# One queue for the early transfers, and new places for the steps that prepare the weights

## The chip, the cores and the metric

The kernel runs on one core of a Trainium2 chip. The metric is the device time of one execution in microseconds (us); lower is better. All inputs lie in the chip's memory (HBM) in the layout that the host has prepared, and the core brings them to its on-chip memory by DMA transfers. A transfer is issued by the queue of an engine; here by SyncE (SP in the rows), which does nothing else, and by ScalarE (ACT), which issues transfers in between its activations, in program order. The other engines are TensorE (PE; PEld are its weight loads), VectorE (DVE) and GpSimd (POOL).

## What is computed

Three stages follow one another, for 4 batches, 8 heads, 768 steps and 48 channels a head:

```python
f = 1.0 / (1.0 + np.exp(-f_logit))                       # stage 1: gated linear attention
for t in range(S):
    state = f[:, :, t, :, None] * state + k_t (x) v_t    # outer product
    y[:, :, t] = q_t @ state
h = xt @ U @ V                                           # stage 2, over time, rank 32; x = y
u = x + h.transpose(0, 2, 1)
x = u + np.maximum(u @ w_ch1, 0.0) @ w_ch2               # 384 -> 1536 -> 384
theta = x @ w_theta                                      # stage 3
y = w_tok_r @ (x * np.cos(theta)) + w_tok_i @ (x * np.sin(theta))
u = x + y
out = u + np.maximum(u @ w_ch, 0.0)
```

The weights come in 64 bits and are turned into 32-bit numbers on the chip; the large products use a high and a low part of each operand, three products instead of one.

## The kernel before

**Attention.** The 768 steps of a batch are cut into 6 chunks of 128 (`c`; over all batches they are numbered `g`, 0 to 23). A chunk has one tile `raw` [128, 3, 4, 128]: the q, k and gate rows of four head pairs, even heads on partitions 0 to 47 and odd heads on 64 to 111. `load_raw(g)` fetches it in two halves of 288 KB, one for each set of partitions; for chunk 0 each half is cut once more so that the gate comes first. Four such tiles are in turn in use by the first batch, so chunk 4 goes into chunk 0's tile and chunk 5 into chunk 1's, once the last reader there is done. `load_v(g)` fetches the chunk's `vt`, three buffers in turn. The memsets ahead of the loads clear partitions 32 to 63 of each `raw` tile on VectorE and GpSimd, and two tiles `first` are filled on VectorE.

For each chunk the steps are: `pre_a` (ScalarE: sigmoid of the gates, L232, and two small copies), `pre_s` (VectorE: the running product of the gates as one scan, L241; GpSimd: q times it, L245), `pre_r` four times (VectorE: reciprocal, L252; GpSimd: k times it, L255), `sc` (TensorE: scores, L266), `mask_` twice (VectorE, L277), `kt` (TensorE: transposes of k, L287; ScalarE copies them), `kv` (TensorE: the chunk's addition to the state; ScalarE copies it, L337; GpSimd adds it up), `xx` (TensorE: the chunk's output, L303 and L309; ScalarE copies it to `xf`, L312, and the state to `wst`, L345), `xt` (TensorE: transposes of `xf`, L354; ScalarE copies them), `au` (TensorE: the product with U, L457). `nxt_load(c)`, right after xx(c), issues load_raw of chunk c + 4 and load_v(c + 3) for the first batch's start. Between the steps of batch 0 stand fillers (`keep_warm`, L450): products whose result nobody uses, in numbers that WARM and KEEP give.

**The order** is written out by hand: the instructions of every engine run in the order in which the steps are called. `attention(0)` gives the list of steps of batch 0 with a weight each; `place` runs through it and puts other steps in at given shares of the sum of weights. Those others are the 15 pieces of weights of stage 2: piece 0 is U, 1 and 2 are the halves of V (96 KB each), 3 to 14 are half matrices of 768 KB, alternately of `w_ch1` and `w_ch2`. A piece has four steps, whose places are the four numbers of its row in WPOS: the load (`w_load`, which calls `w_issue`, L739 on, and `fetch`, L865), the scale (two activations on ScalarE, L869 and L871), the join (two instructions on VectorE, L874 and L877, that make 32 bits of 64) and the store (a copy on ScalarE, L166 for the large pieces and L759 for V, with a subtraction on GpSimd, L163). Places of 1 and more stand in the list after it, `moe1(0)`: stage 2 of batch 0, TensorE products with pieces 3 to 14 as weights (L514, L531, L534), with the attention of batch 1 put in between. APOS gives the places of batch 1's first steps in batch 0's list; LN bounds the lane of `hT` (the product with V, L475) of the second half in moe1(0).

A piece is loaded into a slot: pieces 0 and 8 share slot 0, pieces 1, 2 and 9 slot 1, piece 7 has slot 2; the others are loaded over weight tiles that are filled later.

**Who issues what, before.** In load_raw the first halves go out on SyncE, the second halves of batch 0 on ScalarE, those of later batches on SyncE. `vt` goes out on SyncE. Of the pieces, 0 to 7 go out on ScalarE, 8 to 14 on SyncE. load_raw(0) is called inside the loop of memsets, after the first `raw` tile's; load_raw(1) to load_raw(3) with load_v(0) to load_v(2) after that loop. A step that issues a transfer takes its turn in its engine's order, and waits there for the tile to be free.

Of the kernel before, what the change touches and what calls it, by code (L numbers as in the profile page):

```python
# [15 lines left out]
B, H, S, D = 4, 8, 768, 48  # L16
DM = H * D
DFF = 4 * DM
RANK = 32
CH = 128  # L20
NCH = S // CH
# [4 lines left out]
HT = S // 2  # L26
# [42 lines left out]
W0 = (100, 1200, 800, 600)  # L69

WPOS = (
    (0.1827, 0.1862, 0.3967, 0.3987),
    (0.181, 0.3167, 0.4779, 0.5379),
    (0.1871, 0.3096, 0.78, 0.782),
    (0.1954, 0.3485, 0.781, 0.8798),
    (0.4876, 0.6876, 0.8144, 0.8857),
    (0.3106, 0.4606, 0.8355, 0.9329),
    (0.5676, 0.7591, 0.9091, 0.9916),
    (0.5164, 0.6603, 1.02, 1.059),
    (0.5308, 1.15, 1.155, 1.246),  # L80
    (0.784, 1.028, 1.156, 1.247),
    (1.005, 1.187, 1.206, 1.258),
    (0.9349, 1.215, 1.217, 1.295),
    (1.063, 1.28, 1.413, 1.438),
    (1.248, 1.541, 1.554, 1.584),
    (1.258, 1.625, 1.662, 1.758),
)
LN = (0.01438, 0.1137)
AKNOT = (0.0301, 0.2835, 0.5161, 0.6622, 0.8408)
APOS = (0.8165, 0.9293, 0.9293, 0.9577, 0.9577, 0.999)  # L90
P_MIN = 2.0 ** -60
P_FLOOR = 2.0 ** -80

# [23 lines left out]
def place(main, timed):  # L117

    total = sum(w for w, _ in main)
    todo = sorted(timed, key=lambda x: x[0])  # L120
    i, at = 0, 0.0
    for w, f in main:
        while i < len(todo) and todo[i][0] * total <= at + 0.5 * w:
            todo[i][1]()
            i += 1
        f()
        at += w
    for _, f in todo[i:]:
        f()
# [18 lines left out]
def tile_kernel(ctx: ExitStack, tc: tile.TileContext, qkf, v, U, V, w1, w2, wth, wch, wtok, vT, out):  # L148
    nc = tc.nc
# [6 lines left out]
    const = fast.enter_context(tc.tile_pool(name="const", bufs=1))  # L156
# [39 lines left out]
    raw = [ap_.tile([128, 3, NP, CH], F32, name=f"raw{i}") for i in range(3)]  # L196
# [6 lines left out]
    def rawof(g):  # L203

        return raw[g % 4] if g < NCH else raw[(g - 4) % 3]

    def load_raw(g):
        if g >= B * NCH:
            return
        b, c = divmod(g, NCH)  # L210
        r = rawof(g)
        for i in ((slice(2, 3), slice(0, 2)) if g == 0 else (slice(0, 3),)):
            nc.sync.dma_start(out=r[0:D, i], in_=qkf[b, c, 0, :, i])
            (nc.sync if b else nc.scalar).dma_start(out=r[64:64 + D, i], in_=qkf[b, c, 1, :, i])

    def load_v(g):
        if g >= B * NCH:
            return
        vt = ap_.tile([128, DM], F32, tag="v", bufs=3, name="vt")
        nc.sync.dma_start(out=vt, in_=v[g // NCH, g % NCH])  # L220
        st["v", g] = vt
# [225 lines left out]
    def keep_warm(t, n):  # L447
        o = ps("B1", [128, HT])
        for _ in range(n):
            mm(out=o, lhsT=t[:, 0:128], rhs=t, start=True, stop=True)  # L450
# [34 lines left out]
    def hT_lo(eng, b, th, k):  # L485
        u = xT[b][:, k, HT * th:HT * th + HT]
        sub(eng, st["ul", b, th][:, k], u, f32(st["uh", b, th][:, k]))
# [4 lines left out]
    def prelude_h(b, th):  # L492
        return [(400, lambda k=k: hT(b, th, k)) for k in range(NK)]
# [217 lines left out]
    with tc.manual_schedule():  # L711
# [3 lines left out]
        for r in raw:  # L715
            nc.vector.memset(r[32:64, 0:2], 0.0)
            nc.gpsimd.memset(r[32:64, 2], 20.0)
            if r is raw[0]:
                load_raw(0)
                for t in first:  # L720
                    nc.vector.memset(t, P_FLOOR)
        load_raw(1)
        load_v(0)
        load_raw(2)
# [14 lines left out]
        def w_issue(n):  # L739
            j, h = pieces[n]  # L740
            k = SLOT[n]
            buf = ring[:, 1536 * k:1536 * k + 1536] if k < 3 else const.tile([128, 1536], I32, tag=f"W{k}", name="w64")
            if j == "U":
                return fetch(nc, const, U, [128, NCH * RANK], nc.scalar if n < 8 else nc.sync, buf=buf)
            if j == "V":
                return fetch(nc, const, V[:, HT * h:HT * h + HT], [RANK, HT], nc.scalar, buf=buf[:, S * h:S * h + S])
            sl = slice(768 * h, 768 * h + 768)
            src = w1[j].rearrange("p (k f) -> p k f", k=NK)[:, :, 256 * h:256 * h + 256] if j < 3 else w2[j - 3][:, sl]
            return fetch(nc, const, src, [128, 768], nc.scalar if n < 8 else nc.sync, buf=buf)

        def w_store(n, w):
            j, h = pieces[n]
# [20 lines left out]
        def w_load(n):  # L773
            got[n] = w_issue(n)
# [11 lines left out]
        first_h += [(500, lambda k=k: hT_lo(nc.vector, 0, 0, k)) for k in range(NK)]  # L786
        place(attention(0) + first_h, timed[0] + [(x, f) for x, (_, f) in zip(APOS, ahead)])
        keep_warm(wz, KEEP[9])
        del ahead[:len(APOS)]
        for b in range(B - 1):  # L790
            att, ahead = ahead, attention(b + 2) if b + 2 < B else []
            h1 = (0.04, 0.3) if b else LN[:2]
            lanes = [(*h1, prelude_h(b, 1)), (0.86, 0.92, prelude(b + 1)),
# [9 lines left out]
            out=flag[:, 0:1], in_=pend.rearrange("p g j -> p (g j)"), axis=mybir.AxisListType.X, op=ALU.min  # L803
# [39 lines left out]
def fetch(nc, pool, src, shape, eng, tag=None, bufs=1, parts=((0, None),), buf=None):  # L843

    n = shape[1]  # L850
    if src.dtype == F32:
        w = buf[0:shape[0], 0:n].bitcast(F32) if buf is not None else pool.tile(shape, F32, tag=tag, bufs=bufs, name="w32")
        for o, m in parts:
            dst = w[o:m] if len(src.shape) == 2 else w[o:m].rearrange("p (k n) -> p k n", k=src.shape[1])
            eng.dma_start(out=dst, in_=src)
        return (lambda: None), lambda: w
    if buf is not None:
        t = buf[0:shape[0], 0:2 * n].rearrange("p (n t) -> p n t", t=2)
    else:
        t = pool.tile([shape[0], n, 2], I32, tag=tag, bufs=bufs, name="w64")  # L860
    for o, m in parts:
        dst = t[o:m].rearrange("p n t -> p (n t)")
        if len(src.shape) == 3:
            dst = dst.rearrange("p (k n) -> p k n", k=src.shape[1])
        eng.dma_start(out=dst, in_=src.bitcast(I32))  # L865
    lo, hi = t[:, :, 0], t[:, :, 1]

    def scale():
        nc.scalar.activation(out=hi.bitcast(F32), in_=hi.bitcast(F32), func=ACTF.Copy, scale=2.0 ** -112)  # L869
        top = t.rearrange("p n t -> p (n t)").bitcast(U8)[:, 3:8 * n:8]  # L870
        nc.scalar.activation(out=lo, in_=top, func=ACTF.Copy, scale=1.0 / 32, bias=-15.5 / 32)  # L871

    def join():
        nc.vector.scalar_tensor_tensor(  # L874
            out=lo, in0=hi, scalar=-(2 ** 31), in1=lo, op0=ALU.bitwise_and, op1=ALU.bitwise_or
        )
        nc.vector.scalar_tensor_tensor(  # L877
            out=lo, in0=hi, scalar=3, in1=lo, op0=ALU.logical_shift_left, op1=ALU.bitwise_or
        )
        return lo.bitcast(F32)  # L880

    return scale, join
# [210 lines left out]
```

## Time and profile before

| | |
|---|---|
| time, median of 3 runs | 728.12 us (726.79 to 728.24) |
| the profiled execution | 726.67 us, span from the first to the last instruction 724.9 us |
| TensorE busy | 692.3 us, 96% of the span |
| VectorE, ScalarE, GpSimd busy | 459.1, 298.2, 293.6 us |
| attention(0) | up to 74.75 us, the first product of moe1(0) |
| data moved | 46.14 MB, mean 64 GB/s |

The page's slices cut the span into 40 equal parts of 18.1 us. Digits are tenths: for an engine its busy share, for PEclk the clock that TensorE was granted (9 is full speed, 2.4 GHz; half of it is 1.2 GHz). The timelines give for each row the start, the length, the engine and its line, what was written and read, and in brackets the idle time of that engine just before and what ended it. An engine's name with a q is its queue: there the length is the time from the first issue's start to the last issue's end. In a table by stretches the columns are named in the first group that has one.

### The profile page before, as it was taken

What the parts mean: (1) busy time and instruction counts of PE and PEld (TensorE: products, weight loads), DVE (VectorE), ACT (ScalarE), POOL (GpSimd) and SP (SyncE); (2) the same over time, 40 slices, a digit from 0 to 9 for tenths busy, and PEclk for the clock granted to TensorE, in tenths of its full rate; (3) what the DMA queues carried; (4) which work ended last, traced back from release to release, by engine and by line L of the source; (5) the groups of instructions that cost most, each with busy time, mean ns of one, the idle gap of its engine ahead of it and who ended that gap; (6) DMA issues with size and microseconds to landing.
All of it is one profiled execution on the core that took longest, in us unless ns stands there. A gap on an engine that the chain in (4) does not pass through costs nothing.

```text
span 724.9 us, 12959 instructions
## 1 busy us (share of the span) xinstructions
PE 692.3 (96%) x5221; PEld 652.1 (90%) x5221; DVE 459.1 (63%) x707; ACT 298.2 (41%) x638; POOL 293.6 (41%) x302
## 2 busy tenths in 40 slices
PE   5989999999999999999999999899999999999996
PEld 5766889999999999899999999899989999999996
DVE  7976887765544545544443478779896568459432
ACT  2757574533433324333323377564442233223211
POOL 5446646442432222332221145344574245236212
PEclk8979999999999999999999999999999999999999
DMA  8785524332122222222000244423000100000102
GB/s 163 190 226 134 155 38 121 70 65 44 44 45 45 45 44 44 45 45 44 2 1 1 88 132 131 132 88 89 0 1 23 45 1 19 25 23 1 44 22 71
DMA packets 18004, 46.14 MB, mean 64 GB/s; under 512 B 2288, under 2 KB 8560, under 8 KB 17936
## 3 DMA queue, kind: packets, MB, share of 16 engines
q1 hardware_dynamic: 15760, 39.13, 21.4%
q10 hardware_dynamic: 2176, 6.10, 3.2%
q8 instruction: 43, 0.70, 0.4%
q14 instruction: 25, 0.20, 0.1%
HBM read 40.50 MB, written 4.72 MB: 62 GB/s over the span
## 4 chain that ended last, share of the span: by engine, by line
PE 32%; DVE 11%; issue 6%; POOL 4%; DMA 3%; ACT 3%; SPq 0%; POOLq 0%; DVEq 0%; ACTq 0%
PE ps_A L666 11%; PE ps_A L514 6%; PE ps_B L694 5%; PE ps_A L531 3%; DMA r<-in_wtok_dram 2%; PE ps_B L618 2%; POOL W L163 2%; PE ps_A L534 2%; DVE r L625 1%; DVE r L626 1%; DVE kk L623 1%; DVE z L641 1%; DVE z L642 1%; DVE xT L672 1%; PE ps_B L309 1%
## 5 line engine op out<-in xcount | busy, mean ns | idle before, releaser
L520 DVE SCALAR_TENSOR_TENSOR hl<-ps_A,hh 128x384 fp32r<-128x384 f32 x96 | 53.2, 555 | 142.9 <-ACT hh L519 142.5
L666 PE MATMUL ps_A<-W,zh 128*128 128x384 f32 x576 | 125.3, 338 | 0.7 <-DVE xT L672 0.7
L531 PE MATMUL ps_A<-hh,W 128*128 128x384 f32 x552 | 118.0, 343 | 3.8 <-ACT hh L519 2.7
L514 PE MATMUL ps_A<-uh,W 128*128 128x384 f32 x576 | 119.8, 342 | 0.9 <-ACT uh L481 0.9
L514 PEld LDWEIGHTS ps_A<-uh,W 128*128 128x128 f32 x576 | 99.3, 188 | 3.5 <-ACT uh L481 1.7
L531 PEld LDWEIGHTS ps_A<-hh,W 128*128 128x128 f32 x552 | 94.8, 188 | 7.8 <-ACT hh L519 3.4
L666 PEld LDWEIGHTS ps_A<-W,zh 128*128 128x128 f32 x576 | 100.5, 188 | 1.1 <-DVE xT L672 1.0
L519 ACT ACTIVATE hh<-ps_A 128x384 fp32r<-128x384 f32 x96 | 46.9, 489 | 126.7 <-PE ps_A L514 125.9
L163 POOL TENSOR_TENSOR zl<-z,zh 128x768 fp32r<-128x768 f32 x24 | 44.7, 1861 | 107.1 <-ACT zh L643 97.6
L252 DVE RECIPROCAL f<-p 112x128 f32<-112x128 f32 x96 | 86.9, 929 | 0.9
L666 PE MATMUL ps_A<-W,zl 128*128 128x384 f32 x288 | 73.8, 336 | 1.9 <-POOL zl L163 1.8
L163 POOL TENSOR_TENSOR ul<-xT,uh 128x384 fp32r<-128x384 f32 x45 | 49.2, 1102 | 50.8 <-ACT uh L481 33.6
L255 POOL TENSOR_TENSOR raw<-raw,f 112x256 f32<-112x256 f32 x48 | 37.3, 777 | 77.9 <-DVE f L252 64.1
L514 PE MATMUL ps_A<-ul,W 128*128 128x384 f32 x288 | 66.4, 336 | 0.6 <-POOL ul L163 0.6
L534 PE MATMUL ps_A<-hl,W 128*128 128x384 f32 x276 | 65.5, 335 | 0.0
L245 POOL TENSOR_TENSOR raw<-raw,p 112x512 f32<-112x512 f32 x24 | 30.9, 1288 | 71.5 <-DVE p L241 60.3
L666 PEld LDWEIGHTS ps_A<-W,zl 128*128 128x128 f32 x288 | 51.8, 188 | 3.2 <-POOL zl L163 3.1
L514 PEld LDWEIGHTS ps_A<-ul,W 128*128 128x128 f32 x288 | 51.5, 188 | 1.5 <-POOL ul L163 1.5
L534 PEld LDWEIGHTS ps_A<-hl,W 128*128 128x128 f32 x276 | 49.6, 188 | 0.0
L629 ACT ACTIVATE sh<-r 128x384 f32<-128x384 f32 x24 | 12.6, 525 | 76.7 <-DVE r L626 76.7
L643 ACT ACTIVATE zh<-z 128x768 fp32r<-128x768 f32 x24 | 20.3, 847 | 45.2 <-DVE z L642 45.2
L163 POOL TENSOR_TENSOR W<-r,W 128x384 fp32r<-128x384 f32 x24 | 26.9, 1136 | 29.6 <-ACT W L166 29.6
(167 smaller groups left out, 1250.2 us busy)
## 6 DMA issues: line engine op xcount, KB each, us to landing
raw<-in_qkf_dram SPq DMA_DIRECT2D x41, 288.0 KB, 5.3
r<-in_wtok_dram SPq DMA_DIRECT2D x24, 384.0 KB, 3.6
vt<-in_v_dram SPq DMA_DIRECT2D x24, 192.0 KB, 5.2
out_dram<-o SPq DMA_DIRECT2D x24, 192.0 KB, 1.9
xT<-in_w_dram SPq DMA_DIRECT2D x5, 768.0 KB, 6.1
w<-in_w_dram ACTq DMA_DIRECT2D x4, 768.0 KB, 8.8
w<-in_w_dram SPq DMA_DIRECT2D x2, 768.0 KB, 5.8
raw<-in_qkf_dram ACTq DMA_DIRECT2D x5, 288.0 KB, 7.3
```

Of the source, the lines that this page charges most:

```text
L163: eng.tensor_tensor(out=out_, in0=a, in1=b, op=ALU.subtract)
L245: nc.gpsimd.tensor_tensor(out=x, in0=x, in1=p, op=ALU.mult)
L252: nc.vector.reciprocal(out=f[:, j], in_=p[:, j])
L255: nc.gpsimd.tensor_tensor(out=x, in0=x, in1=f[:, j - 1:j + 1], op=ALU.mult)
L514: mm(out=t, lhsT=w1t(lo, fb)[:, k, 128 * fo:128 * fo + 128], rhs=x[:, k], start=(n == 0), stop=(n == 8))
L519: nc.scalar.activation(out=hh, in_=t, func=ACTF.Relu)
L520: nc.vector.scalar_tensor_tensor(out=hl, in0=t, scalar=0.0, in1=f32(hh), op0=ALU.max, op1=ALU.subtract)
L531: mm(out=st["acc"][k], lhsT=w2t(lo, fb)[:, fo, 128 * k:128 * k + 128], rhs=hh, start=(first_of(f) and lo == 0), stop=False)
L534: mm(out=st["acc"][k], lhsT=w2t(0, fb)[:, fo, 128 * k:128 * k + 128], rhs=hl, start=False, stop=last_of(f))
L643: nc.scalar.activation(out=zh, in_=z, func=ACTF.Copy)
L666: mm(out=t, lhsT=z[:, i, 128 * k:128 * k + 128], rhs=w[:, S * i + HT * th:S * i + HT * th + HT], start=(s == 0 and n == 0), stop=(s == NCH ...
L694: mm(out=t, lhsT=w[:, k, 128 * m:128 * m + 128], rhs=x[:, k], start=(n == 0), stop=(n == 8))
```

## The change

load_raw issues the second halves of chunks 0 and 1 on ScalarE and of all others on SyncE. All pieces go out on SyncE. load_raw(0) is called after the loop of memsets, and the `first` tiles are filled after the second `raw` tile's memset instead of the first's. In WPOS the rows of pieces 0 to 8 and of 12 and 13 have other places: the V halves' loads stand ahead of U's, piece 4's and piece 5's earlier, piece 7's after piece 8's, and the steps that follow the loads move by a slot or a few. The first step of batch 1 (APOS) moves from ahead of kv(4) to ahead of mask_(4). LN's bounds shift by 0.0006 and 0.001.

```diff
--- before.py
+++ after.py
@@ -69,25 +69,25 @@
 W0 = (100, 1200, 800, 600)
 
 WPOS = (
-    (0.1827, 0.1862, 0.3967, 0.3987),
-    (0.181, 0.3167, 0.4779, 0.5379),
-    (0.1871, 0.3096, 0.78, 0.782),
-    (0.1954, 0.3485, 0.781, 0.8798),
-    (0.4876, 0.6876, 0.8144, 0.8857),
-    (0.3106, 0.4606, 0.8355, 0.9329),
-    (0.5676, 0.7591, 0.9091, 0.9916),
-    (0.5164, 0.6603, 1.02, 1.059),
-    (0.5308, 1.15, 1.155, 1.246),
+    (0.1874, 0.1909, 0.4014, 0.4034),
+    (0.181, 0.3167, 0.4779, 0.5602),
+    (0.1685, 0.32, 0.78, 0.782),
+    (0.191, 0.3441, 0.7819, 0.8957),
+    (0.4428, 0.6428, 0.7829, 0.8967),
+    (0.2879, 0.4379, 0.8154, 0.9102),
+    (0.5815, 0.7263, 0.923, 1.006),
+    (0.5425, 0.6864, 1.046, 1.085),
+    (0.5308, 1.153, 1.155, 1.246),
     (0.784, 1.028, 1.156, 1.247),
     (1.005, 1.187, 1.206, 1.258),
     (0.9349, 1.215, 1.217, 1.295),
-    (1.063, 1.28, 1.413, 1.438),
-    (1.248, 1.541, 1.554, 1.584),
+    (1.096, 1.28, 1.413, 1.438),
+    (1.248, 1.547, 1.549, 1.579),
     (1.258, 1.625, 1.662, 1.758),
 )
-LN = (0.01438, 0.1137)
+LN = (0.01383, 0.1147)
 AKNOT = (0.0301, 0.2835, 0.5161, 0.6622, 0.8408)
-APOS = (0.8165, 0.9293, 0.9293, 0.9577, 0.9577, 0.999)
+APOS = (0.7623, 0.9293, 0.9293, 0.9577, 0.9577, 0.999)
 P_MIN = 2.0 ** -60
 P_FLOOR = 2.0 ** -80
 
@@ -211,7 +211,7 @@
         r = rawof(g)
         for i in ((slice(2, 3), slice(0, 2)) if g == 0 else (slice(0, 3),)):
             nc.sync.dma_start(out=r[0:D, i], in_=qkf[b, c, 0, :, i])
-            (nc.sync if b else nc.scalar).dma_start(out=r[64:64 + D, i], in_=qkf[b, c, 1, :, i])
+            (nc.scalar if g < 2 else nc.sync).dma_start(out=r[64:64 + D, i], in_=qkf[b, c, 1, :, i])
 
     def load_v(g):
         if g >= B * NCH:
@@ -715,10 +715,10 @@
         for r in raw:
             nc.vector.memset(r[32:64, 0:2], 0.0)
             nc.gpsimd.memset(r[32:64, 2], 20.0)
-            if r is raw[0]:
-                load_raw(0)
+            if r is raw[1]:
                 for t in first:
                     nc.vector.memset(t, P_FLOOR)
+        load_raw(0)
         load_raw(1)
         load_v(0)
         load_raw(2)
@@ -741,12 +741,12 @@
             k = SLOT[n]
             buf = ring[:, 1536 * k:1536 * k + 1536] if k < 3 else const.tile([128, 1536], I32, tag=f"W{k}", name="w64")
             if j == "U":
-                return fetch(nc, const, U, [128, NCH * RANK], nc.scalar if n < 8 else nc.sync, buf=buf)
+                return fetch(nc, const, U, [128, NCH * RANK], nc.sync, buf=buf)
             if j == "V":
-                return fetch(nc, const, V[:, HT * h:HT * h + HT], [RANK, HT], nc.scalar, buf=buf[:, S * h:S * h + S])
+                return fetch(nc, const, V[:, HT * h:HT * h + HT], [RANK, HT], nc.sync, buf=buf[:, S * h:S * h + S])
             sl = slice(768 * h, 768 * h + 768)
             src = w1[j].rearrange("p (k f) -> p k f", k=NK)[:, :, 256 * h:256 * h + 256] if j < 3 else w2[j - 3][:, sl]
-            return fetch(nc, const, src, [128, 768], nc.scalar if n < 8 else nc.sync, buf=buf)
+            return fetch(nc, const, src, [128, 768], nc.sync, buf=buf)
 
         def w_store(n, w):
             j, h = pieces[n]
```

## Rows read from the trace of the kernel before

**Rows 1.** Page, granted TensorE clock in 40 equal slices, tenths.
```profile
PEclk8979999999999999999999999999999999999999
```

**Rows 2.** Stretches: us, busy PE, PEld, DVE, ACT, POOL (count), clock, DMA share, GB/s.
```profile
13.52:20.35 6.83, 5.70 (x28) 5.18 (x29) 6.79 (x9) 1.48 (x4) 4.34 (x5) 0.50 0.76 144
...
44.24:54.48 10.24, 9.96 (x88) 8.04 (x90) 9.02 (x12) 5.25 (x10) 3.42 (x5) 0.50 0.63 160
...
75.00:180.00 105.00, 103.12 (x925) 96.80 (x925) 76.01 (x107) 54.05 (x111) 50.70 (x52) 1.00 0.35 84
...
18.00:25.00 7.00, 6.94 (x59) 5.83 (x59) 6.90 (x10) 2.38 (x8) 3.40 (x5) 0.83 0.40 101
...
25.00:45.00 20.00, 16.79 (x234) 12.63 (x231) 15.64 (x20) 15.89 (x38) 10.20 (x16) 0.98 0.98 267
0.00:45.00 45.00, 33.73 (x333) 27.61 (x334) 35.64 (x45) 21.86 (x52) 23.10 (x41) 0.92 0.85 200
```

**Rows 3.** TensorE's timeline: first scores, fillers behind them, fillers before moe1(0).
```profile
13.46 1.21 PE L266 MATMUL ps_A<-raw 48*128 48x128 f32 x8 [3.34 <-POOL raw L255]
...
17.65 4.09 PE L450 MATMUL ps_B<-wz 128*128 128x384 f32 x15
...
69.50 3.88 PE L450 MATMUL ps_B<-wz 128*128 128x384 f32 x19
```

**Rows 4.** TensorE's timeline, 33 to 57 us: xt(1), kt(3), xt(2), kt(4), xt(3).
```profile
34.18 0.55 PE L354 MATMUL ps_A<-ident,xf 128*128 128x128 f32 x3 [0.25 <-ACT xf L312]
...
40.30 0.55 PE L287 MATMUL ps_A<-ident,raw 112*128 112x112 f32 x4
...
44.46 0.90 PE L354 MATMUL ps_A<-ident,xf 128*128 128x128 f32 x3 [2.84 <-ACT xf L312]
...
54.93 0.55 PE L287 MATMUL ps_A<-ident,raw 112*128 112x112 f32 x4
...
56.17 0.55 PE L354 MATMUL ps_A<-ident,xf 128*128 128x128 f32 x3
```

**Rows 5.** VectorE's timeline, 0 to 12 us: last memset, first scan.
```profile
5.67 0.91 DVE L716 MEMSET raw<- 32x1024 f32 x1 [0.16 <-issue]
9.51 1.23 DVE L241 TENSOR_TENSOR_SCAN p<-f,first 112x512 f32<-112x512 f32 x1 [2.93 <-ACT f L234]
```

**Rows 6.** ScalarE's timeline, 0 to 12 us: issues, chunk 0's sigmoid.
```profile
2.31 5.93 ACTq L214 DMA_DIRECT2D raw<-in_qkf_dram  x2
8.36 0.63 ACT L232 ACTIVATE f<-raw 112x512 f32<-112x512 f32 x1 [6.12 <-DMA raw<-in_qkf_dram]
```

**Rows 7.** Issues, KB each, us to landing: at 1.28, 31.66, 33.55, 35.67 us.
```profile
raw<-in_qkf_dram SPq DMA_DIRECT2D x1, 96.0 KB, 2.7
...
raw<-in_qkf_dram SPq DMA_DIRECT2D x1, 288.0 KB, 6.0
...
raw<-in_qkf_dram ACTq DMA_DIRECT2D x1, 288.0 KB, 9.0
...
xT<-in_w_dram ACTq DMA_DIRECT2D x1, 768.0 KB, 14.5
```

**Rows 8.** SyncE's waits, 0 to 75 us: total, times, longest us.
```profile
SPq L220 <- DMA raw<-in_qkf_dram: 4.2, 1, 4.2
```

**Rows 9.** Timelines of both issuing queues: the two halves of chunk 5.
```profile
31.66 0.31 SPq L213 DMA_DIRECT2D raw<-in_qkf_dram  x1
...
33.55 0.32 ACTq L214 DMA_DIRECT2D raw<-in_qkf_dram  x1
```

**Rows 10.** ScalarE's timeline, 36 to 57 us: copies, chunk 5, piece 7.
```profile
37.32 1.67 ACT L759 ACTIVATE vs<-xT 32x384 fp32r<-32x384 f32 x3
39.01 0.33 ACT L337 ACTIVATE kvs<-ps_A 112x192 f32<-112x192 f32 x1
42.60 0.63 ACT L232 ACTIVATE f<-raw 112x512 f32<-112x512 f32 x1 [3.26 <-DMA raw<-in_qkf_dram]
...
50.23 0.95 ACT L869 ACTIVATE xT<-xT 128x768 f32<-128x768 f32 x1 [4.25 <-DMA xT<-in_w_dram]
```

## The prediction, made before the change was run

> **What bounds the kernel now.** I read the page's slices first, then a table by stretches, then each engine's timeline in the stretch that stood out. Everything that the change touches runs in the first 180 us. After the first slices TensorE's granted clock stands at 9 throughout [rows 1], and from 75 us on it is busy for 103.12 of 105 us at a clock of 1.00 [rows 2]. There it bounds the kernel, and work that starts earlier at 75 us ends earlier by as much. What can be won lies ahead of 75 us, in attention(0), and the dips of the clock digits say where: two stretches at 0.50, from 13.52 to 20.35 us and from 44.24 to 54.48 us [rows 1, 2]. Each follows an idle time of TensorE: 3.34 us before 13.46, 2.84 us before 44.46 [rows 3, 4].
>
> The first idle time is the end of a start-up chain: sigmoid of chunk 0 on ScalarE, scan on VectorE, product on GpSimd, first scores on TensorE. The scan starts at 9.51 and waited 2.93 us for ScalarE, though VectorE's last memset had ended at 6.58 [rows 5]. ScalarE's sigmoid stands at 8.36, after 6.12 us of idleness [rows 6]. Its data had long landed: chunk 0's third of 96 KB, issued at 1.28 us, took 2.7 us [rows 7], so 3.98. What held it is in the line above it: ScalarE's own queue was in transfer issues from 2.31 to 8.24 [rows 6], and the last of these waited. [...]
>
> The second is one late transfer. Chunk 5's first half was issued by SyncE at 31.66, its second half by ScalarE only at 33.55 [rows 9], since there it stands behind the activations ahead of it in order. They took 6.0 and 9.0 us to land [rows 7], so 37.7 and 42.6; the sigmoid stood from 39.34 to 42.60 for it [rows 10], `xf` behind it, and TensorE's transposes behind that until 44.46 [rows 4]. Then the clock was halved.
>
> **The change, part by part.** *Start.* ScalarE keeps three issues (chunk 0 twice, chunk 1), all before 2.3 us; the one at the end of the 5.93 us row goes to SyncE. The sigmoid can start at about 4.1 and its three activations end by 5.3 (8.36 to 9.51 is 1.15 us [rows 5, 6]). VectorE still has all its memsets ahead, ending at 6.58, so the scan starts at 6.65 instead of 9.51: -2.86. Chunk 1 is no longer behind half of chunk 2, and its memset comes before the two `first` memsets. Bounds: 0, if chunk 0 lands as late as the old sigmoid, to -2.93, the wait itself. I take -2.86, because the landing has its row.
>
> *First half clock.* The 15 fillers took 4.09 us; 19 at full clock took 3.88 [rows 3], so 15 cost 3.06: up to -1.03. TensorE's idle time before 13.46 shrinks from 3.34 to 0.5, but the work there stays thin. Between 0 and -1.03 I take half, -0.5.
>
> *Chunk 5.* Both halves now go out on SyncE as soon as chunk 1's buffer is free, at 31.66 less 3.4, so 28.3; piece 4 and all later ones stand behind them. Landing by the old 6.0 us after issue: 34.3, with 9.0: 37.3. The sigmoid's turn: ScalarE's V copies took 1.67 and the `kv` copy 0.33, to 39.34 [rows 10]; the change swaps these two, same sum. Less 3.4 that is 36.0. So the wait is 0 at best and 1.3 at worst; I take 0, since what shared the engines during the 9.0 us (pieces 4, 5 and 8) is behind it or gone ahead. TensorE's 2.84 us goes: it is its own order that is late next.
>
> *Second half clock.* From `xt` of one chunk to the `kt` two chunks on, TensorE took 40.30 - 34.18 = 6.12 us at full clock and 54.93 - 44.46 = 10.47 at half [rows 4]: -4.35, if the clock stays; bounds 0 and -4.35.
>
> *What is late next.* Pieces 4, 7 and 6 now arrive through SyncE's one queue, and ScalarE scales all three before it copies `xf` of chunk 3, for which TensorE's next `xt` waits. ScalarE was busy 5.25 us in the half-clock stretch [rows 2]; a third pair of scale activations (one took 0.95 [rows 10]) adds 1.9: 7.15 from `xt` to `xf`, where TensorE needs 6.12 and 56.17 - 54.93 = 1.24 [rows 4], 7.36. Even, so nothing as long as the pieces are there: piece 6 by about 43.5. By sizes 9.6 MB go ahead of its end. The old kernel moved 200 GB/s over the first 45 us, 9.0 MB, with only 101 GB/s from 18 to 25 us, where little was queued, and 267 GB/s from 25 to 45 with the DMA engines 0.98 busy [rows 2]. SyncE fills that hole now (chunk 4's halves leave together at about 15, where its second half had waited for ScalarE): 7 us x 166 GB/s = 1.2 MB. Then 9.6 MB are through at 45 - 0.6 / 0.267 = 42.8, and land about a microsecond later. That is a tie with 43.5. Piece 7 took 14.5 us to land in the old order and ScalarE stood 4.25 us for it [rows 7, 10], so this wait is real: bounds 0 and +4.25; nearest to the tie I take +1.0, with the earlier sigmoid of chunk 6 in it, which stands at the end of the same queue and ahead of a `kt` copy.
>
> *The queue.* Twelve issues move to SyncE, each about 0.32 us as in both queues' rows [rows 9]. SyncE goes in order: `v3` waits for xx(0) and `v4` for xx(1), and behind them now stand pieces 5, 4, 8, 7 and 6. Until xx(0), at about 22, what is already issued (through chunk 4, 4.7 MB) lasts to 24.6 at the same rates, so the wait is covered; without that cover piece 6 would be late by what the engines idle.
>
> The Trainium skill's page "DMA: Bandwidth & Descriptors", section "Issuing engines are not separate DMA queues", says that transfers run on the same 16 DMA engines whichever engine started them, so that the issuer only saves issue time. By it the move of chunk 5 wins nothing in bandwidth, and the sum would be the first two terms alone. The rows give it more, because the move also changes what stands ahead.
>
> *Moved steps.* Most WPOS changes are by one slot. VectorE's order of scans, reciprocals, masks and joins stays; stores of pieces 3 to 5 stay ahead of moe1(0), whose first weights they are; piece 6's store moves to its first step and is used two steps on. Pieces 7 and 12 move one slot later with users far off, and the other slots of moe1(0) don't change. LN shifts no step over another group. Nothing for all of these; the cover is VectorE's and ScalarE's slack (76.01 and 54.05 busy of 105 us [rows 2]), and without it a late weight stops TensorE by as much.
>
> Sum: -2.86 - 0.5 - 2.84 - 4.35 + 1.0 = -9.55. The profiled execution is 726.67 us (span 724.9): 717.1. The median of the runs shown is 1.45 above it, 728.12: **718.6**. With the best ends 717.0; with the waits at +2.5 720.1.
>
> **The rivals.**
> *The clock falls again.* TensorE's work between 10 and 20 us and around xt(2) stays thin, and a wait of 2 us for pieces 7 or 6 comes where the 2.84 us was. Then the 4.35 is not won: 722.9. For it: both old dips follow a gap. Against: the stretch between them kept the clock with gaps of 0.25 us [rows 4], and I expect gaps of under 1.
>
> *The bytes bind, not the queue.* From 25 to 45 us the engines are 0.98 busy [rows 2]; if chunk 5 and the pieces come no sooner relative to their users, the wait and the clock stay and only the start is won: 728.12 - 3.4 = 724.7. Its rule is that of the section named above. Against: the pieces issued beside chunk 5 stand behind it now.
>
> *Slower: one queue holds the pieces back.* If SyncE sits in a wait for a buffer while ScalarE needs piece 6, ScalarE stands in order, `xf` behind it, and TensorE behind that. The old `xt` of chunk 3 is at 56.17 [rows 4]; with another halved stretch (4.35) and ScalarE's 2.4 us after the landing, break-even is piece 6 landing at 49.5, that is 9.6 MB at 194 GB/s. The old mean was 200 [rows 2], so the margin hangs on the hole being filled. Landing at 52.5 gives about +3: 731.
>
> *It does not act.* The start could still be set by VectorE's memsets and piece U, which ScalarE scales early and now gets third in line, and the rest be given back in moe1(0): 728.
>
> **How the numbers follow.** Forecast 0.62, clock again 0.16, bytes 0.10, no effect 0.04, slower 0.08. A measurement of this kernel can tell about 0.2% (1.5 us) from no change. Faster: 0.62 + 0.16 + 0.10 = 0.88; same 0.04; slower 0.08. Range: 715.5 (the best ends and a little of moe1(0)) to 724.5, which takes in the second case and most of the third, about 0.8 of the chance.
>
> **What would show it.** The scan at about 6.7; first scores at 10.6; no TensorE gap over 1 us around 38; the granted clock at 1.00 from 20 to the end; the first moe1 matmul at 65 instead of 74.75. I am wrong if ScalarE's scale of piece 7 or 6 shows a wait of over 2 us for a landing, if a third stretch at 0.50 appears, or if TensorE has new gaps after 65 us.

## The result, and the profile after

| | before | after |
|---|---|---|
| median, 4 runs each | 727.55 us (726.79 to 728.24) | 717.05 us (715.27 to 720.02) |
| ratio after to before, 95% interval | | 0.986 (0.982 to 0.990) |
| the profiled execution | 726.67 us, span 724.9 | 715.27 us, span 713.5 |
| first product of moe1(0) | 74.75 us | 64.83 us |

The clock row of after's page, for [rows 1]:

```profile
PEclk9999999999999999999999999999999999999999
```

The table by stretches of after, for [rows 2] and with its columns:

```profile
18.00:25.00 7.00, 6.65 (x85) 4.93 (x85) 6.79 (x10) 4.27 (x12) 4.35 (x6) 1.00 1.04 256
25.00:45.00 20.00, 19.12 (x267) 13.97 (x267) 19.44 (x27) 18.02 (x38) 13.27 (x19) 1.00 0.96 279
75.00:180.00 105.00, 103.18 (x929) 97.14 (x928) 74.48 (x105) 51.03 (x106) 49.89 (x54) 1.00 0.33 73
```

In this execution no stretch stands at 0.50 until the work ends, the hole from 18 to 25 us is filled (256 GB/s for 101), and from 25 to 45 us TensorE is busy for 19.12 us instead of 16.79 and VectorE for 19.44 instead of 15.64, at nearly the same rate of transfers (279 GB/s for 267). The stretch from 75 us on is as it was.

TensorE's timeline of after, for [rows 3, 4]: first scores, the product with U of chunk 0, xt(1), xt(2), kt(4), xt(3), first product of moe1(0).

```profile
10.92 0.72 PE L266 MATMUL ps_A<-raw 48*128 48x128 f32 x8
...
29.62 0.83 PE L457 MATMUL ps_A<-xf,u 128*32 128x384 f32 x2 [0.68 <-ACT u L754]
30.39 0.55 PE L354 MATMUL ps_A<-ident,xf 128*128 128x128 f32 x3
...
37.86 0.55 PE L354 MATMUL ps_A<-ident,xf 128*128 128x128 f32 x3
...
43.97 0.55 PE L287 MATMUL ps_A<-ident,raw 112*128 112x112 f32 x4
...
45.92 0.55 PE L354 MATMUL ps_A<-ident,xf 128*128 128x128 f32 x3 [0.64 <-ACT xf L312]
...
64.83 1.37 PE L514 MATMUL ps_A<-uh,W 128*128 128x384 f32 x3 [0.85 <-ACT uh L481]
```

The first product of moe1(0) in before:

```profile
74.75 1.90 PE L514 MATMUL ps_A<-uh,W 128*128 128x384 f32 x6 [0.85 <-ACT uh L481]
```

VectorE's timeline of after, the first scan, for [rows 5]:

```profile
6.61 1.23 DVE L241 TENSOR_TENSOR_SCAN p<-f,first 112x512 f32<-112x512 f32 x1
```

ScalarE's timeline of after, for [rows 6, 10]: the sigmoid of chunk 0, the scale of U, the sigmoid of chunk 5, the scales of pieces 7 and 6.

```profile
4.07 0.63 ACT L232 ACTIVATE f<-raw 112x512 f32<-112x512 f32 x1 [1.82 <-DMA raw<-in_qkf_dram]
...
19.98 0.39 ACT L869 ACTIVATE xT<-xT 128x192 f32<-128x192 f32 x1 [4.18 <-DMA xT<-in_U_dram]
...
35.80 0.63 ACT L232 ACTIVATE f<-raw 112x512 f32<-112x512 f32 x1
...
41.88 0.98 ACT L869 ACTIVATE xT<-xT 128x768 f32<-128x768 f32 x1
...
43.78 0.95 ACT L869 ACTIVATE w<-w 128x768 f32<-128x768 f32 x1
```

The waits of 3.26 us for chunk 5 and of 4.25 us for piece 7 are gone: the last three rows have no bracket. Piece 7's issue on SyncE's timeline of after:

```profile
30.61 0.55 SPq L865 DMA_DIRECT2D xT<-in_w_dram  x1
```

The issues of after with KB each and us to landing, piece 7 and then piece 6 (`w`), for [rows 7]:

```profile
xT<-in_w_dram SPq DMA_DIRECT2D x1, 768.0 KB, 9.0
w<-in_w_dram SPq DMA_DIRECT2D x1, 768.0 KB, 11.8
```

Piece 7 lands at 39.6, 10.6 us sooner than before, and piece 6, issued at 31.21, at 43.0.

### The profile page after: what moved, and what is told of

Same layout as the page of the kernel before. It is cut to its first block, busy times and chain, and to the rows that moved or that the text cites. A ratio compares the mean times of both kernels' runs of the same rounds, so it can differ in the third digit from the quotient of the medians.

```text
span 713.5 us, 12957 instructions
## 1 busy us (share of the span) xinstructions
PE 686.3 (96%) x5221; PEld 647.2 (91%) x5221; DVE 458.8 (64%) x707; ACT 298.1 (42%) x638; POOL 294.2 (41%) x302
## 4 chain that ended last, share of the span: by engine, by line
PE 39%; DVE 11%; issue 4%; POOL 2%; ACT 2%; DMA 2%; SPq 0%; DVEq 0%; POOLq 0%; ACTq 0%
PE ps_A L666 11%; PE ps_A L514 9%; PE ps_B L694 5%; PE ps_A L531 5%; PE ps_B L618 2%; PE ps_A L534 2%; DMA r<-in_wtok_dram 2%; DVE r L625 2%; DVE kk L623 1%; DVE r L626 1%; DVE z L641 1%; DVE z L642 1%; POOL W L163 1%; DVE xT L672 1%; DVE sh L639 1%
## 5 line engine op out<-in xcount | busy, mean ns | idle before, releaser
L531 PE MATMUL ps_A<-hh,W 128*128 128x384 f32 x552 | 118.1, 343 | 2.6 <-ACT hh L519 1.9
L531 PEld LDWEIGHTS ps_A<-hh,W 128*128 128x128 f32 x552 | 94.8, 188 | 6.7 <-ACT hh L519 2.5
L163 POOL TENSOR_TENSOR ul<-xT,uh 128x384 fp32r<-128x384 f32 x45 | 49.5, 1109 | 51.6 <-ACT uh L481 34.5
L643 ACT ACTIVATE zh<-z 128x768 fp32r<-128x768 f32 x24 | 20.3, 847 | 45.1 <-DVE z L642 45.1
```

Source lines behind the costliest of these rows:

```text
L163: eng.tensor_tensor(out=out_, in0=a, in1=b, op=ALU.subtract)
L531: mm(out=st["acc"][k], lhsT=w2t(lo, fb)[:, fo, 128 * k:128 * k + 128], rhs=hh, start=(first_of(f) and lo == 0), stop=False)
L643: nc.scalar.activation(out=zh, in_=z, func=ACTF.Copy)
```

## The experiments

The theory after the result was the prediction's own: start, chunk 5's second half and the clock carry the gain. The rival: the pieces carry it, since ScalarE's next wait was the one for piece 7. "Before" and "after" below name the two kernels; ratios are to runs of before on the same chip.

### One part alone, in the kernel before

**The start: b_start.** Second halves of chunks 2 and 3 go to SyncE.

```diff
-            (nc.sync if b else nc.scalar).dma_start(out=r[64:64 + D, i], in_=qkf[b, c, 1, :, i])
+            (nc.scalar if g in (0, 1, 4, 5) else nc.sync).dma_start(out=r[64:64 + D, i], in_=qkf[b, c, 1, :, i])
```

> The kernel before, with only the second halves of chunks 2 and 3 moved to SyncE (chunks 0, 1, 4 and 5 stay on ScalarE, as do the pieces). Theory (the start is set by ScalarE's issues): the first scan starts at 6.6 us instead of 9.51, first scores at 10.6 to 11.0, the stretch at half clock before 20 us goes, and the first product of moe1(0) moves by the start alone, 3 to 4 us: 723.5 to 724.5. Chunk 5 still comes late: the sigmoid waits 2 to 4 us and the second half-clock stretch stays. Rival (the start is hidden behind the later waits): time within 1 us of the kernel before, 727 to 728, with the same first scan at 6.6.

Measured: 724.82 us (721.36 to 726.11), ratio 0.996 (0.9939 to 0.9981). ScalarE's timeline of b_start, the scale of piece 7:

```profile
47.05 0.93 ACT L869 ACTIVATE xT<-xT 128x768 f32<-128x768 f32 x1 [4.69 <-DMA xT<-in_w_dram]
```

TensorE's, xt(3):

```profile
50.94 0.90 PE L354 MATMUL ps_A<-ident,xf 128*128 128x128 f32 x3 [2.67 <-ACT xf L312]
```

Two stretches of b_start, in the columns of [rows 2]:

```profile
9.46:20.35 10.89, 9.97 (x92) 8.29 (x93) 10.75 (x14) 2.54 (x7) 6.90 (x10) 1.00 1.01 186
...
50.41:60.66 10.25, 9.45 (x78) 7.46 (x80) 9.58 (x10) 6.53 (x15) 4.99 (x4) 0.50 0.13 31
```

The early start is real and its halved stretch is gone. But ScalarE then stands 4.69 us for piece 7, TensorE 2.67 us behind it, and the halved stretch comes later. The time lies just above the theory's range.

**Chunk 5's second half: b_chunk5.** Those of chunks 4 and 5 go to SyncE.

```diff
-            (nc.sync if b else nc.scalar).dma_start(out=r[64:64 + D, i], in_=qkf[b, c, 1, :, i])
+            (nc.scalar if g < 4 else nc.sync).dma_start(out=r[64:64 + D, i], in_=qkf[b, c, 1, :, i])
```

> The kernel before, with only the second halves of chunks 4 and 5 moved to SyncE. Theory of the prediction's terms (the wait for chunk 5 and the clock are one cause): the 3.26 us wait of the sigmoid goes, TensorE's 2.84 us gap goes, the clock stays, 2.84 + 4.35 = 7.2 us are won: 720.3. Rival 1 (a second bound stands right behind: piece 7, which landed at 50.2 us, holds ScalarE, and with it the copy of xf and TensorE's xt(3), until 55.3 instead of 56.17): only about 1 us is won, 726 to 727. Rival 2 (the bytes bind): the second half of chunk 5 lands at 41 us or later and nothing is won.

Measured: 725.79 us (723.31 to 730.53), ratio 0.9984 (0.9962 to 1.0006). ScalarE's timeline of b_chunk5, the scale of piece 7:

```profile
47.84 0.94 ACT L869 ACTIVATE xT<-xT 128x768 f32<-128x768 f32 x1 [3.25 <-DMA xT<-in_w_dram]
```

TensorE's, xt(2), xt(3) and kv(4):

```profile
42.03 0.55 PE L354 MATMUL ps_A<-ident,xf 128*128 128x128 f32 x3
...
51.76 0.55 PE L354 MATMUL ps_A<-ident,xf 128*128 128x128 f32 x3 [2.30 <-ACT xf L312]
...
56.73 0.67 PE L334 MATMUL ps_A<-vt,ktok 128*64 128x48 f32 x16 [2.25 <-ACT ktok L289]
```

A stretch of b_chunk5:

```profile
57.67:64.50 6.83, 6.77 (x58) 4.67 (x58) 3.82 (x3) 4.73 (x13) 2.69 (x3) 0.50 0.69 184
```

xt(2) comes without a wait, 2.43 us sooner, and the gap returns before xt(3), behind piece 7, as rival 1 had it. No gain that can be told.

**The clock alone: b_fill.** Fourteen fillers bridge TensorE's wait before xt(2).

```diff
+                if c == 2:
+                    warm(14)
```

> The kernel before, with 14 fillers more right ahead of xt(2): TensorE works through the 2.84 us in which it stood for chunk 5, and the wait itself stays. Theory (the granted clock alone costs 4.35 us there): no stretch at half clock after 20 us, time 723.2. Rival (piece 7's landing at 50.2 us holds ScalarE and sets xt(3) whatever TensorE's clock): the stretch is at full clock, but xt(3) comes at about 55.3 and the time is 726.5 to 727.5. If the clock falls nevertheless, the fillers cost nothing or up to 2.8 us.

Measured: 725.40 us (724.31 to 726.45), ratio 0.9976 (0.9961 to 0.9992). Stretches of b_fill:

```profile
44.24:54.48 10.24, 8.57 (x107) 6.46 (x105) 8.75 (x12) 4.87 (x8) 3.97 (x5) 1.00 0.70 179
59.49:66.32 6.83, 6.77 (x57) 4.56 (x56) 3.88 (x4) 4.57 (x12) 2.78 (x3) 0.50 0.68 178
```

TensorE's timeline of b_fill, kv(4):

```profile
58.68 0.67 PE L334 MATMUL ps_A<-vt,ktok 128*64 128x48 f32 x16 [2.30 <-ACT ktok L289]
```

The clock holds where it fell in [rows 2], and falls after the next gap; the time lies between theory and rival. So each of the prediction's three terms is there, yet each alone is given back, wholly or for the greater part, in the stretch where ScalarE waits for piece 7 and TensorE then for ScalarE.

### One part undone, in the kernel after

**The places: a_old_places.** WPOS, LN and APOS as before.

```diff
-    (0.1874, 0.1909, 0.4014, 0.4034),
...
-LN = (0.01383, 0.1147)
-APOS = (0.7623, 0.9293, 0.9293, 0.9577, 0.9577, 0.999)
+    (0.1827, 0.1862, 0.3967, 0.3987),
...
+LN = (0.01438, 0.1137)
+APOS = (0.8165, 0.9293, 0.9293, 0.9577, 0.9577, 0.999)
```

> The changed kernel with WPOS, LN and APOS of the kernel before: the queue change alone. Theory (the queues make the gain, the places of the steps are worth nothing by themselves): 716.5 to 718. Rival (the places are needed, since the transfers land in another order): ScalarE stands for piece 4 or 7 or for V, and the time is 719 to 722.

Measured: 717.85 us (715.69 to 719.13), ratio 0.9868 (0.9834 to 0.9901). The places are worth nothing that can be told.

**The memsets' order: a_old_memset.** load_raw(0) and the `first` fills stand after the first `raw` tile's memset again.

```diff
-            if r is raw[1]:
+            if r is raw[0]:
+                load_raw(0)
...
-        load_raw(0)
```

> The changed kernel with the memsets in the old order: the first tiles filled after the first raw tile, load_raw(0) called there. Theory (VectorE is without a gap from 6.6 us to 60, so what delays its second scan delays all): chunk 1's first half is issued at about 4.5 instead of 3.22 us and lands at about 11.2 instead of 9.94, the second scan starts at about 12.4 instead of 11.18, and the time is 0.8 to 1.3 us longer, about 718. Rival (the later slack takes it): no difference to the changed kernel.

Measured: 715.15 us (714.59 to 717.01), ratio 0.9832 (0.9816 to 0.9849). No loss; the second scan starts at 11.17 us, in after at 11.18.

**The halves of chunks 2 to 5: a_raw_act.** They go back to ScalarE.

```diff
-            (nc.scalar if g < 2 else nc.sync).dma_start(out=r[64:64 + D, i], in_=qkf[b, c, 1, :, i])
+            (nc.sync if b else nc.scalar).dma_start(out=r[64:64 + D, i], in_=qkf[b, c, 1, :, i])
```

> The changed kernel with the second halves of chunks 2 to 5 on ScalarE again (pieces stay on SyncE). Theory (ScalarE's issue of chunk 3, which waits for an earlier landing, sets the first scan, and the second halves come late there): first scan at 9 us or later, a half-clock stretch before 20 us, the sigmoid of chunk 5 waits again; of the 10 us 3 to 5 are kept: 722 to 725. Rival (once the pieces stand behind on SyncE, chunk 5 comes in time from either queue): only the start is lost, 719.5 to 721.

Measured: 716.75 us (715.57 to 717.40), ratio 0.9851 (0.9834 to 0.9869): the whole gain stays. ScalarE's timeline of a_raw_act, its issues, chunk 0's and chunk 5's sigmoid:

```profile
3.92 0.79 ACTq L214 DMA_DIRECT2D raw<-in_qkf_dram  x2
4.75 0.63 ACT L232 ACTIVATE f<-raw 112x512 f32<-112x512 f32 x1 [2.51 <-POOL mask masks.py:66]
...
38.60 0.63 ACT L232 ACTIVATE f<-raw 112x512 f32<-112x512 f32 x1 [1.21 <-DMA raw<-in_qkf_dram]
```

VectorE's, the first scan:

```profile
6.61 1.23 DVE L241 TENSOR_TENSOR_SCAN p<-f,first 112x512 f32<-112x512 f32 x1
```

Both sides of the expectation missed. ScalarE's fourth issue comes at 3.92 us (2.31 in before), but its fifth and last is through by 4.7 us, where before needed until 8.24 [rows 6]; the sigmoid at 4.75 still comes before VectorE is through with its memsets, so the start isn't lost. Chunk 5's sigmoid stands for only 1.21 us.

**The pieces: a_pieces_act.** Pieces 0 to 7 go back to ScalarE; all else stays as in after.

```diff
-                return fetch(nc, const, U, [128, NCH * RANK], nc.sync, buf=buf)
+                return fetch(nc, const, U, [128, NCH * RANK], nc.scalar if n < 8 else nc.sync, buf=buf)
...
-            return fetch(nc, const, src, [128, 768], nc.sync, buf=buf)
+            return fetch(nc, const, src, [128, 768], nc.scalar if n < 8 else nc.sync, buf=buf)
```

> The changed kernel with pieces 0 to 7 issued by ScalarE again (halves of chunks 2 to 5 stay on SyncE, new places stay). Theory (piece 7's landing is the second bound, and SyncE's early issue of the pieces is what takes it away): the start is won (scan 6.6 us) and chunk 5 comes in time, but piece 7 lands at 45 us or later instead of 39.65, ScalarE stands 2 to 5 us for it, xt(3) comes at 49 to 51 instead of 45.9, a half-clock stretch follows, and the time is 721 to 725. Rival (who issues the pieces is indifferent): within 1.5 us of the changed kernel, 716 to 718.5.

Measured: 726.82 us (723.15 to 733.14), ratio 1.0007 (0.9977 to 1.0036): the whole gain is gone, more than expected. ScalarE's timeline of a_pieces_act, the scales of U and piece 6:

```profile
22.76 0.39 ACT L869 ACTIVATE xT<-xT 128x192 f32<-128x192 f32 x1 [6.47 <-DMA xT<-in_U_dram]
...
51.83 0.92 ACT L869 ACTIVATE w<-w 128x768 f32<-128x768 f32 x1 [3.27 <-DMA w<-in_w_dram]
```

TensorE's, xt(0) and xt(3):

```profile
25.20 0.55 PE L354 MATMUL ps_A<-ident,xf 128*128 128x128 f32 x3 [1.95 <-ACT xf L312]
...
53.98 0.64 PE L354 MATMUL ps_A<-ident,xf 128*128 128x128 f32 x3 [3.73 <-ACT xf L312]
```

Stretches of a_pieces_act:

```profile
27.00:33.82 6.82, 6.76 (x76) 5.28 (x72) 6.75 (x11) 5.07 (x12) 3.73 (x7) 0.50 0.42 149
54.30:64.54 10.24, 10.18 (x92) 8.10 (x90) 6.36 (x7) 4.52 (x12) 3.47 (x3) 0.50 0.38 110
```

The early scan stays and chunk 5 is in time, but ScalarE stands for pieces, TensorE's gaps follow, and two stretches at 1.2 GHz follow those. With a_raw_act this says what carries the gain: which queue the pieces are in. How large the loss is belongs to this kernel alone, because the new places were made for SyncE: with them U stands third among ScalarE's pieces and is waited for 6.47 us. With the old places, the early start and the pieces on ScalarE, b_start took 724.82 us.

### The pieces' queue alone, in the kernel before

**All of them: b_pieces_sp.** Pieces 0 to 7 on SyncE, nothing else changed.

```diff
-            return fetch(nc, const, src, [128, 768], nc.scalar if n < 8 else nc.sync, buf=buf)
+            return fetch(nc, const, src, [128, 768], nc.sync, buf=buf)
```

(and the same for U and V)

> The kernel before with one edit: all pieces 0 to 7 are issued by SyncE; the halves of chunks 2 to 5 stay on ScalarE, memsets and places stay. Theory A (the pieces' early issue is the gain, because it fills the stretch from 18 to 25 us and brings piece 7 before ScalarE needs it): DMA over 200 GB/s from 18 to 25 us, piece 7 landed by about 41, no wait of ScalarE for it, no halved clock after 25 us; the old start (scan 9.5, halved clock before 20 us) stays or is made up for, so 718 to 721 us. Theory B (the start and chunk 5's halves are needed too, as the prediction had it): chunk 5's second half still lands at 40 or later, TensorE idle for over 2 us before xt(2), halved clock behind it, 723 to 726.

Measured: 719.00 us (718.63 to 719.40), ratio 0.9893 (0.9869 to 0.9918), after beside it 0.9861. Piece 7 is issued at 32.80 and lands at 41.9 with no wait for it; TensorE's gap before xt(2) is 1.17 us. By the time, piece 7 and the clock after 25 us this is theory A, but its reason fails: the hole from 18 to 25 us is not filled (149 GB/s, where over 200 was expected). Theory B's late second half of chunk 5 is there too, a wait of 1.87 us for ScalarE's sigmoid at 40.29, and costs little.

**Some of them: b_late_sp.** Pieces 4, 6 and 7 on SyncE. (The expectation names piece 0 too; in the kernel it stayed on ScalarE, as the edit shows.)

```diff
-                return fetch(nc, const, U, [128, NCH * RANK], nc.scalar if n < 8 else nc.sync, buf=buf)
+                return fetch(nc, const, U, [128, NCH * RANK], nc.scalar, buf=buf)
...
-            return fetch(nc, const, src, [128, 768], nc.scalar if n < 8 else nc.sync, buf=buf)
+            return fetch(nc, const, src, [128, 768], nc.scalar if n in (3, 5) else nc.sync, buf=buf)
```

> The kernel before with pieces 0, 4, 6 and 7 issued by SyncE; pieces 1, 2 (V), 3 and 5 stay on ScalarE. Theory A (filling 18 to 25 us is what counts): half of the early pieces still stand behind activations, so the mean from 18 to 25 us stays under 200 GB/s, piece 7 lands at 44 or later with a wait of ScalarE of over 1 us: 722 to 726. Theory B (only the order of issue of pieces 4, 7 and 6 counts): piece 7 lands by 41 with no wait: 718 to 721.

Measured: 720.22 us (716.75 to 722.44), ratio 0.9897 (0.9855 to 0.9940). The hole, in the table by stretches of b_late_sp:

```profile
18.00:25.00 7.00, 6.97 (x50) 6.04 (x48) 6.90 (x10) 2.35 (x8) 3.51 (x5) 0.72 0.42 110
```

Piece 7, issued at 34.49, among its issues:

```profile
xT<-in_w_dram SPq DMA_DIRECT2D x1, 768.0 KB, 8.5
```

It lands at 43.0, ScalarE scales it at 43.99 and doesn't wait. The hole is as empty as before and most of the gain is there: theory B by the time and by the missing wait, though the piece lands 2 us later than that theory had it.

**One transfer: b_seven_sp.** Piece 7 alone on SyncE.

```diff
-            return fetch(nc, const, src, [128, 768], nc.scalar if n < 8 else nc.sync, buf=buf)
+            return fetch(nc, const, src, [128, 768], nc.scalar if n < 7 else nc.sync, buf=buf)
```

> The kernel before with one transfer moved: piece 7 is issued by SyncE, all else is as it was. Theory A (piece 7 landed at 50.21 us because the two halves of chunk 6, issued 3.6 us after it on the other queue, landed ahead of it at 46.77 and 48.52): now it stands ahead of them in SyncE's own queue, is issued at about 34 and lands by 45, ScalarE's wait of 4.25 us for it is gone; chunk 5's late second half, the old start and some halved clock before 45 us stay, and piece 6 (ScalarE, issued about 42) may be waited for by 1 to 2 us: 720 to 724 us. Theory B (single waits give nothing, since each is taken up by the next one, as when only chunk 5 or only the clock was mended): piece 6 lands at 51 or later, ScalarE waits for it by over 2 us, xt(3) after 52 us: 725 to 728.

Measured: 721.52 us (720.61 to 725.07), ratio 0.992 (0.9893 to 0.9948). In before, SyncE issued chunk 6's halves 3.6 and 4.0 us after ScalarE's piece 7 [rows 7], and they landed first, at 46.8 and 48.5, the piece at 50.2. In ScalarE's own queue piece 4, which is scaled after it, stood ahead of it: issued at 35.27, landed at 45.1. Piece 4 among the issues of before:

```profile
w<-in_w_dram ACTq DMA_DIRECT2D x1, 768.0 KB, 9.8
```

SyncE's timeline of before:

```profile
39.26 0.33 SPq L213 DMA_DIRECT2D raw<-in_qkf_dram  x1
39.64 0.42 SPq L214 DMA_DIRECT2D raw<-in_qkf_dram  x1
```

The same two among the issues of before, with the mean us to landing:

```profile
raw<-in_qkf_dram SPq DMA_DIRECT2D x2, 288.0 KB, 8.2
```

With piece 7 ahead of them in one queue, SyncE's timeline of b_seven_sp has its issue:

```profile
33.16 0.72 SPq L865 DMA_DIRECT2D xT<-in_w_dram  x1
```

Among its issues, with us to landing:

```profile
xT<-in_w_dram SPq DMA_DIRECT2D x1, 768.0 KB, 8.1
```

ScalarE's timeline, its scale:

```profile
43.96 0.91 ACT L869 ACTIVATE xT<-xT 128x768 f32<-128x768 f32 x1
```

TensorE's next gap, before kv(4):

```profile
54.63 0.66 PE L334 MATMUL ps_A<-vt,ktok 128*64 128x48 f32 x16 [2.12 <-ACT ktok L289]
```

The stretch after that gap:

```profile
55.66:62.49 6.83, 6.77 (x58) 4.77 (x58) 4.36 (x5) 4.84 (x12) 2.47 (x3) 0.50 0.73 201
```

Issue 2.5 us sooner and transfer 6.4 us shorter, so it lands at 41.3 for 50.2; chunk 6 lands 1.2 and 1.6 us later, and ScalarE doesn't wait for it. Piece 4 lands 1.5 us later, at 46.6, and ScalarE waits 0.87 us for it. The edit does two things at once: it puts piece 7 ahead of chunk 6 in one queue and takes it from behind piece 4 in the other; no run parts them. This one edit gives 0.8% of the 1.4%. What it lacks against after is the start (first scores at 13.07 us, then a halved stretch) and what the last rows show: ahead of `ktok` ScalarE stands 2.30 us for GpSimd's sum `kvs` (at 51.21) and 0.46 us for piece 6, still in its own queue, so TensorE has 2.12 us of gap and a halved stretch.

The Trainium skill's page "DMA: Bandwidth & Descriptors", section "Queues, rings and completion order", says that each DMA engine takes turns between the queues that have work for it, while transfers of one queue start in order. The two landings of piece 7, 14.5 us behind piece 4 in the second queue and 8.1 us ahead of chunk 6 in the first, agree with it; no run here shows the turns themselves.

### The changed kernel again, and one step on

**after_again**: the changed kernel, unedited.

> The changed kernel as it is, beside the other two on the same chip: 715 to 719 us under every theory. In its profile the stretch of halved clock around 461 us, which some variants showed and others did not, may or may not be there; with it some 1 to 2 us more.

Measured: 717.64 us (714.24 to 718.35), ratio 0.9861 (0.9825 to 0.9897). Two stretches of its profile, which the first profile of after didn't have:

```profile
13.58:16.99 3.41, 3.41 (x15) 3.41 (x14) 3.41 (x6) 1.48 (x4) 2.09 (x4) 0.50 0.97 170
460.72:464.14 3.42, 3.42 (x11) 3.42 (x12) 3.38 (x8) 1.65 (x4) 2.46 (x2) 0.50 0.00 0
```

The profiles of a_raw_act, a_old_places and a_old_memset (717.4, 717.4 and 717.0 us) have a halved stretch near 461 us as well; those of after (715.27) and a_less_fill (712.51) have none.

**a_less_fill**: nine fillers fewer before moe1(0); nobody uses their results.

```diff
-KEEP = (15, 1, 1, 1, 1, 1, 0, 3, 16, 0)
+KEEP = (15, 1, 1, 1, 1, 1, 0, 3, 7, 0)
```

> The changed kernel with 7 instead of 16 fillers ahead of hT: a version meant to be faster than both. Theory (TensorE works through 19 fillers, 3.88 us, to 63.45 us, while ScalarE's last copy for hT ends at 61.44): nine fillers less are 1.8 us, the first product of moe1(0) comes at about 63.0 instead of 64.83, time 715.3. Rival (weights of moe1(0) or the clock are next): less than 0.7 us, or a new half-clock stretch after 60 us and a loss of 1 to 3 us.

Measured: 712.23 us (711.94 to 713.60), ratio 0.9798 (0.9780 to 0.9817): the fastest of all. TensorE, the fillers and the first product of moe1(0):

```profile
59.47 2.34 PE L450 MATMUL ps_B<-wz 128*128 128x384 f32 x10
...
63.64 1.55 PE L514 MATMUL ps_A<-uh,W 128*128 128x384 f32 x4 [1.30 <-ACT uh L481]
```

Nine fillers less are 9 x 3.88 / 19 = 1.84 us; the gap that opens takes 0.45 back, the rest is small shifts, and moe1(0) starts 1.19 us sooner than at 64.83. The profiled executions differ by 2.76 us, so 1.57 us come after that, 0.80 of them by TensorE's product at 460.08 in after, which had waited 1.26 us and here waits 0.42. Why that wait is shorter was not tested. The time lies 3.1 us below the forecast of 715.3, and the fillers don't explain that part.

## Why the prediction was right, and where it was not

The forecast was 718.6 us and 717.05 was measured; the profiled execution was put at 717.1 and took 715.27. Compared at the same TensorE instructions of both profiles, its terms measured as follows.

| step | predicted | measured, from |
|---|---|---|
| start | -2.86 | -2.54: first scores 13.46 to 10.92 |
| first half clock | -0.5 | -1.25: xt(1) 34.18 to 30.39 is -3.79 |
| chunk 5 | -2.84 | -2.81: xt(2) 44.46 to 37.86 is -6.60 |
| second half clock | -4.35 | -4.36: kt(4) 54.93 to 43.97 is -10.96 |
| what is late next | +1.0 | +1.04: moe1(0) 74.75 to 64.83 is -9.92 |
| after that | 0 | -1.48: the span, 724.9 to 713.5 |

The sizes were right nearly throughout, because each was read as the length of a stretch on TensorE. That the fifth agrees is luck. It was put there for the landing of pieces 7 and 6, and ScalarE waits for neither: what TensorE waits for is ScalarE's own work, 0.64 us before xt(3) behind three pairs of scales, and 0.50 us before the product with U at 58.51. The prediction had called that work even with TensorE's. The last line was not foreseen: 0.9 us of it are the same wait of L531, 2.16 us long in before (at 471.69) and 1.26 in after (at 460.08). after_again, whose wait there was 1.91 us and was followed by 1.2 GHz, shows that this part differs between executions; so does the first half clock. That term was also too narrow: its best end took the fillers alone, -1.03, but the scores behind them (21.67 in before, 16.76 in after) stood at -4.91, 2.37 beyond the start. By xt(1) 1.12 of it was gone again: TensorE waited for ScalarE 0.29 us before xt(0) and 0.68 us before the product with U (29.62), and had waited for neither in before. ScalarE had stood 4.18 us for U's landing (19.98); whether an earlier U would keep some of the 1.12 us was not run.

*Where the reasons failed.* The step "Chunk 5" gave the second gap, and with it the halved stretch, to the move of chunk 5's second half. a_raw_act, with that half on ScalarE, keeps the whole gain, and b_chunk5, with that half moved alone, has none that can be told. The gain hangs on the pieces, which the prediction had only under "what is late next", as a price. There it had read the right rows: it called ScalarE's wait for piece 7 real. What it missed is that this wait, 4.25 us in before, was already the second bound under both gaps. The terms are not independent sums; while piece 7 lands at 47 us or later (b_start, b_chunk5), each of them returns as a gap before xt(3). The first product of moe1(0) shows it without what comes later:

| profile | moe1(0) at, us | from there to the end, us |
|---|---|---|
| before | 74.75 | 650.2 |
| b_start | 73.24 | 651.1 |
| b_chunk5 | 74.99 | 648.7 |
| b_fill | 76.98 | 647.0 |
| a_pieces_act | 76.33 | 648.5 |
| b_seven_sp | 72.95 | 648.4 |
| b_late_sp | 68.92 | 650.7 |
| b_pieces_sp | 67.12 | 649.7 |
| a_raw_act | 65.44 | 650.2 |
| after | 64.83 | 648.7 |

Of the three cures of the first wait only b_start shortens attention(0), by 1.5 us. The last column answers the prediction's "ends earlier by as much": the rest differs by up to 4 us between these profiles, in large part by the wait of L531 near 460 to 472 us (2.16 us in before, 1.15 in b_chunk5, 0.42 in b_fill) and the clock after it. So a gain of 1 or 2 us in a time need not come from attention(0).

*The hole.* "The margin hangs on the hole being filled" is wrong: at 110 GB/s from 18 to 25 us b_late_sp has 720.22. b_seven_sp has its 0.8% with 121 GB/s there and 268 from 25 to 45 us, where before has 101 and 267. The place in the queue did it, not bytes per us. The estimate for piece 6, landing about a microsecond after 42.8, was met at 43.0 and ScalarE asked for it at 43.78, the forecast tie.

*The start.* The scan at 6.61 was forecast as 6.65, by way of the last ScalarE issue going to SyncE. That does it in b_start, but isn't needed: in a_raw_act the same issues on ScalarE are through by 4.7 us. In b_pieces_sp, which has load_raw(0) in its old place among the memsets, they are not: ScalarE is in the last two of its five from 2.29 us on for 5.65 us, much as in [rows 6], and the first scan starts at 9.20. So the place of load_raw(0) does it too, or the places of the pieces, the two things in which these kernels differ; which, and why, was not tested. That an issue can stand until an earlier transfer has landed is in [rows 8]; for ScalarE's issues the traces show only how long they took. The second half of the step, chunk 1's memset, is worth nothing once the halves of chunks 2 and 3 are on SyncE (a_old_memset).

*Moved steps* at nothing were right (a_old_places).

*The rivals.* "The bytes bind" fell: 267 and 279 GB/s from 25 to 45 us are nearly the same, and the time isn't. By the section of the Trainium skill that it rested on ("Issuing engines are not separate DMA queues") a new issuer brings no bandwidth, and the rows agree; what it brought was an order. "The clock falls again" didn't come true in after, but is what b_start, b_chunk5, b_fill and b_seven_sp did: a gap of 2.12 to 2.67 us on TensorE with a halved stretch at or after it. "Slower" had its break-even at piece 6 landing at 49.5; it landed 6.5 us ahead of that. In a_pieces_act it landed at 51.8 and the time was that of before, where the sum would give some 2 us more.

## What to carry to other kernels

When a wait on the bounding engine is to go, look for the transfer that the same feeding engine waits for next, and mend both: here three cures of the first wait gave 0.2 to 0.4% each, one of them within the noise, and one transfer's place behind the second gave 0.8%. Let transfers stand in one queue in the order in which they are needed; in two queues a later transfer of the one can land ahead of an earlier one of the other, as chunk 6 did ahead of piece 7. Compare kernels at an instruction behind the stretch that was changed, and not by the whole time alone. Read each term's size from the stretch it would remove, but test who carries it by undoing one part at a time in the faster kernel.

## What the hardware showed that was not expected

A transfer issued 3.6 us later on the other queue landed 3.4 us earlier (chunk 6's first half and piece 7); the earlier one, behind another 768 KB in its own queue, took 14.5 us, and 8.1 in the other queue ahead of chunk 6. From 25 us on, TensorE's granted clock stood at 0.50 after gaps of 1.91 (after_again, 460.71) to 3.73 us (a_pieces_act); after 1.17 us (b_pieces_sp, xt(2)) and 1.26 us (after, 460.08) it stayed at 1.00, and gaps of 2.16 us in before (471.69) and of 2.30 us in b_chunk5 (xt(3)) left it at 1.00. In the thin work ahead of 20 us a shorter one was enough, 1.63 us before 12.90 in after_again, where 1.32 us in after was not. So a gap of about 2 us goes either way, and the same kernel shows a halved stretch in one execution and not in the next.
